# Attention and expert layer on one core: three tiles of two experts computed during the attention, PSUM tiles shared anew, all in one list schedule

## The chip, the cores and the metric

The kernel runs on one core of a Trainium2 chip. The core has five engines that run their own instruction streams side by side: TensorE (PE, matmuls; PEld is its weight load), VectorE (DVE), ScalarE (ACT), GpSimd (POOL) and SyncE (SP). All of a core's transfers share 16 DMA engines. The metric is device time in microseconds (us) of one execution; lower is better.

## The reference

Eight batches, 8 heads, 576 positions, head size 64. Two attentions are added: one over q, k and v averaged over groups of four positions (144 positions, repeated back to 576), one over a band of the positions nearer than four. The result, 4608 tokens of 512 values, goes through an expert layer: each token goes to one of eight experts.

```python
out = np.repeat(sm_attn(q_d, k_d, v_d), 4, axis=2) + sm_attn_band(q, k, v)   # |i-j| < 4
x = out.transpose(0, 2, 1, 3).reshape(4608, 512)
logits = x @ w_gate
e_idx = np.argmax(logits, axis=1)
gate_w = softmax(logits)[arange, e_idx]
eom = sigmoid(x @ w_output_gate)
for e in range(8):
    mask = e_idx == e
    h = np.maximum(x[mask] @ w1[e], 0.0)          # 512 -> 1024
    out[mask] = gate_w * eom[:, e] * (h @ w2[e])  # 1024 -> 512
```

## The kernel before

The program has two phases, and they don't overlap.

**The attention** is cut into 32 units (a batch's heads two by two: `prep`, `scores`, `values`), with a gate step after each batch (`gate`). All of it is put in as tasks with an engine, a duration and dependencies; `Plan.order` simulates a list schedule of them, and the kernel is written out in that order, so each engine runs its tasks strictly in it. A task's priority is ten times its slot plus a number from the table `AT`. A unit is, with the names that the tasks have and the lines of the profile:

- Tq, Tk: TensorE turns q and k into PSUM (L396), DVE copies them out (qT, kT, L402), POOL averages them (qs, qd, ks, kd, L410 to L418); VD: TensorE averages v (L433), ACT copies (vd, L439).
- DS, LS: the two score matmuls (L455 and L468/L478) into the one PSUM tile S (two banks; columns 0 to 290 of each bank for the band, the rest for the averaged scores). ED, EL: ACT takes exp of the two parts (L460, L484).
- V1: averaged values and their denominators (L503) into the one PSUM tile PD; V2: the band's denominators (L512), also into PD; V3: the band's values (L524) into the one tile PL. S, PD and PL have two banks each, the ring T of turned tiles has two of one bank: all eight banks.
- LND, LN: ACT takes the log of the two denominators (L537, L532), LX: their reciprocal by exp (L540). M2 and M1: DVE multiplies (xd L547, xl L554). ADD: POOL adds (xT L565), CAST: POOL casts (L568).
- Per batch: GL (logits, L601), GT, a chain of short DVE steps, RK (ranks, L633 to L639), INV (which token goes to which place, L686), acc; GX0 to GX2 turn the batch's tokens back (L706), ACT and DVE copy them (xh), `put` (L715) writes 576 rows to the table `hx_xs` in memory.

q and k come a batch at a time (one transfer each, L359, on POOL's queue), v a unit at a time on SP's queue. The weights of three experts are loaded during the attention, in three ring places.

**The experts** begin when all eight batches are in the table. `fetch(e)` gathers five tiles of 128 rows (an indirect DMA each, L774, on POOL); `turn` turns them (L785); `up` makes 64 matmuls U of 320 columns (L794), with a relu on ACT or DVE (L797, L799); `down` makes eight matmuls Y of 512 columns for each tile (L804), ACT scales (y, L806), POOL scatters the rows to the output (L807). Eight experts have five tiles each, so there are 40. Loads of w for expert e+3 stand on POOL's queue behind the scatters of expert e. A loop at the end handles experts with more than 640 tokens; it doesn't run with these inputs.

Of the kernel before, what the change touches and what calls it, by code (L numbers as in the profile page):

```python
# [58 lines left out]
class Task:  # L59

    def __init__(self, kind, slot, eng, dur, fn, deps, uses, mode, lat):
        self.kind, self.slot, self.eng, self.dur, self.fn = kind, slot, eng, dur, fn
# [4 lines left out]
class Plan:

    HOP = 0.10
    SWITCH = 0.13  # L70
# [32 lines left out]
    def order(self):  # L103
        free, mode, wait = {}, None, {}
# [7 lines left out]
        while len(seq) < len(self.tasks):  # L112
# [44 lines left out]
def kernel(  # L157
# [85 lines left out]
    r_qk = [ring(sbA, [HB, H, 8 * D], F16, f"qk{i}", 2) for i in range(2)]  # L243
# [27 lines left out]
    t_ks = add("c1", 0, "DVE", 1.0, c_ks)  # L271
# [8 lines left out]
    t_band = add("c2", 0, "POOL", 1.5, c_band)  # L280
# [9 lines left out]
    t_mk = add("c3", 0, "DVE", 1.0, c_mk, deps=[t_band])  # L290
# [28 lines left out]
    t_pv = add("c4", 0, "DVE", 4.6, c_pv, deps=[t_pb])  # L319
# [5 lines left out]
    t_wg0 = add("c5", 4, "DVE", 0.5, c_late, deps=[t_id])  # L325
# [4 lines left out]
    t_wg = add("c5", 5, "SP", 1.0, c_wg, deps=[t_wg0], lat=2.0)  # L330
# [9 lines left out]
    t_cg = add("c5", 4, "POOL", 2.0, c_gate)  # L340
# [6 lines left out]
    t_rev = add("c5", 5, "DVE", 0.6, c_rev, deps=[t_cg])  # L347
# [35 lines left out]
    def prep(u):  # L383
# [4 lines left out]
        for i, nm in enumerate("qk"):  # L388
# [32 lines left out]
            e2 = add("kd" if i else "qd", n, "POOL", 1.4 if i else 0.9, fn, deps=[ev, t_ks], uses=[xT, s2, sd])  # L421
# [5 lines left out]
        def fn(T=T):  # L427
            for blk in range(3):
                for s in range(2):
                    for h in range(2):  # L430
                        g = 2 * blk + s
                        r0 = 64 * h + 32 * s
                        nc.tensor.matmul(T.tile[r0:r0 + 32, D * blk:D * blk + D], lhsT=pv[:, g, :],  # L433
                                         rhs=vbuf.tile[:, min(g, NB - 1), h, :], start=(blk == 0), stop=True,
                                         skip_group_check=True)
# [479 lines left out]
```

## Time and profile before

| | us |
|---|---|
| median of three runs | 441.91 (437.96 to 444.44) |
| the profiled execution | 438.84, its span 437.0 |
| TensorE busy | 347.9 (80% of the span) |
| VectorE, ScalarE, GpSimd busy | 222.0 (51%), 180.7 (41%), 261.4 (60%) |
| mean granted clock of TensorE | 0.902 |

The span is the time from the first to the last instruction; 1.84 us of the execution lie around it. [...] A busy share is an average over two phases that have different limits.

### The profile page before, as it was taken

The numbers are of one execution on the slowest core, as the hardware profiler recorded it, in microseconds if no ns is written. First come the engines' busy times: TensorE is split into PE (matmuls) and PEld (weight loads), VectorE is DVE, ScalarE is ACT, GpSimd is POOL, SyncE is SP. The second block draws the span as 40 slices with busy tenths as digits, with TensorE's granted clock in tenths as the row PEclk, the third lists the DMA queues.
The fourth block names the chain that finished last, engine by engine and source line by source line (L and its number), as shares of the span: only waits on it lengthen the run. The fifth ranks groups of instructions, "written<-read, shape, count | busy, mean of one in ns | idle before, by whom it ended". The sixth has DMA issues, their size and how long they took to land.

```text
span 437.0 us, 14182 instructions
## 1 busy us (share of the span) xinstructions
PE 347.9 (80%) x6105; PEld 244.9 (56%) x6105; DVE 222.0 (51%) x550; ACT 180.7 (41%) x369; POOL 261.4 (60%) x363
## 2 busy tenths in 40 slices
PE   1268879779868968689788544699999999999990
PEld 0256657567656756567567332356565665656640
DVE  8343578387677487696967661233242332323210
ACT  1045654454545555456656420123333343343430
POOL 8375976755956668767684317517485755842330
PEclk9998997686977889989999855889999999999996
DMA  6994499961898655994330113315988989891221
GB/s 105 183 168 76 79 163 190 182 112 39 164 190 138 148 102 89 213 189 111 70 79 7 56 54 92 91 39 136 230 187 231 162 241 223 197 235 60 84 75 47
DMA packets 79113, 57.21 MB, mean 131 GB/s; under 512 B 49341, under 2 KB 71357, under 8 KB 79040
## 3 DMA queue, kind: packets, MB, share of 16 engines
q0 software_dynamic: 30240, 40.94, 46.9%
q1 hardware_dynamic: 48800, 15.26, 16.8%
q8 instruction: 50, 0.82, 0.7%
q14 instruction: 23, 0.19, 0.2%
HBM read 68.21 MB, written 15.22 MB: 191 GB/s over the span
## 4 chain that ended last, share of the span: by engine, by line
PE 39%; DVE 16%; POOL 16%; issue 12%; DMA 8%; ACT 5%; POOLq 1%; DVEq 0%; ACTq 0%
PE U L794 12%; PE Y L804 10%; PE PD L503 4%; POOL xT L565 3%; DMA w<-in_moe_w_dram 3%; DMA qk<-in_k_dram 3%; PE PD L512 3%; POOL out_dram L807 3%; DVE kT L402 2%; DVE xl L554 2%; PE T L706 2%; POOL kd L418 2%; DVE xd L547 2%; ACT r L540 2%; DVE g_og L644 2%
## 5 line engine op out<-in xcount | busy, mean ns | idle before, releaser
L807 POOL DMA_INDIRECT out_dram<-y,sidx x40 | 39.7, 993 | 64.8 <-ACT y L806 35.0
L794 PE MATMUL U<-xgT,w 128*128 128x320 f16 x512 | 75.5, 310 | 3.6 <-issue 1.4
L804 PE MATMUL Y<-w,hs 128*128 128x512 f16 x320 | 73.8, 379 | 0.0
L794 PEld LDWEIGHTS <-w 128*128 128x128 f16 x512 | 51.8, 101 | 27.1 <-issue 4.2
L799 DVE TENSOR_SCALAR hs<-U 128x320 f16<-128x320 f32 x64 | 31.4, 492 | 68.5 <-PE U L794 57.2
L565 POOL TENSOR_TENSOR xT<-xl,xd 128x576 f32<-128x576 f32 x32 | 38.7, 1210 | 24.8 <-DVE xl L558 24.2
L774 POOL DMA_INDIRECT xg<-hx_xs,gidx x40 | 40.7, 1018 | 21.3 <-issue 11.3
L797 ACT ACTIVATE hs<-U 128x320 f16<-128x320 f32 x64 | 27.9, 437 | 59.2 <-PE U L794 58.0
L806 ACT ACTIVATE y<-Y,xg 128x512 f32<-128x512 f32 x40 | 27.5, 688 | 55.7 <-PE Y L804 38.0
L804 PEld LDWEIGHTS <-hs 128*128 128x128 f16 x320 | 30.5, 98 | 31.5
L503 PE MATMUL PD<-e,vd 64*128 64x144 f32 x384 | 40.6, 352 | 5.3 <-DVE xd L547 4.3
L396 PE MATMUL T<-id,qk 72*64 72x72 f16 x1024 | 28.8, 214 | 19.3 <-DMA qk<-in_q_dram 14.0
L537 ACT ACTIVATE r<-PD 64x144 f32<-64x144 f32 x64 | 18.3, 286 | 55.9 <-PE PD L512 55.5
L547 DVE TENSOR_TENSOR xd<-PD,r 64x144 f32<-64x144 f32 x64 | 19.5, 305 | 42.0 <-ACT r L540 33.0
L410 POOL TENSOR_TENSOR ks<-kT 128x288 f32<-128x288 f16 x32 | 21.9, 685 | 28.9 <-DVE kT L402 28.7
L396 PEld LDWEIGHTS <-qk 72*64 72x64 f16 x1024 | 23.8, 124 | 26.6 <-DMA qk<-in_q_dram 14.2
L503 PEld LDWEIGHTS PD<-e,vd 64*128 64x128 f32 x384 | 32.7, 230 | 7.8 <-issue 2.8
L786 DVE COPY xgT<-T 128x1024 f16<-128x1024 f16 (+1 forms) x24 | 14.4, 602 | 42.3 <-PE T L785 39.5
L418 POOL TENSOR_TENSOR kd<-ks 64x192 f16<-64x192 f32 x64 | 32.3, 505 | 4.4
L402 DVE COPY kT<-T 128x576 f16<-128x576 f16 x32 | 24.1, 754 | 17.4 <-PE T L396 17.2
L524 PE MATMUL PL<-e,v 64*64 64x57 f32 (+1 forms) x1280 | 28.6, 232 | 1.1 <-issue 0.9
L402 DVE COPY qT<-T 128x576 f16<-128x576 f16 x32 | 23.9, 749 | 9.4 <-PE S L478 5.0
(120 smaller groups left out, 580.6 us busy)
## 6 DMA issues: line engine op xcount, KB each, us to landing
w<-in_moe_w_dram POOLq DMA_DIRECT2D x16, 1024.0 KB
v<-in_v_dram SPq DMA_DIRECT2D x128, 80.0 KB, 5.6
hx_xs<-xh SPq DMA_DIRECT2D x8, 578.2 KB, 4.8
qk<-in_q_dram POOLq DMA_DIRECT2D x7, 576.0 KB
qk<-in_k_dram POOLq DMA_DIRECT2D x7, 576.0 KB
xg<-hx_xs,gidx POOLq DMA_INDIRECT x40
out_dram<-y,sidx POOLq DMA_INDIRECT x40
qk<-in_q_dram POOLq DMA_DIRECT2D x1, 432.0 KB
```

The lines of the kernel that those rows point to most:

```text
L396: nc.tensor.transpose(t16[64 * h:64 * h + 64, HB * c:HB * c + HB], src.tile[:, 2 * hp + h, D * c:D * c + D], id16[0:HB, 0:HB])
L402: nc.vector.tensor_copy(xT.tile.rearrange("p (n c) -> p n c", c=8), T.tile.bitcast(F16)[:, 0:S].rearrange("p (c n) -> p n c", c=8))
L418: nc.gpsimd.tensor_tensor(o.rearrange("p b (s x) -> p b s x", s=2), _ap(t, [t.ap[0], [114, 3], [58, 2], [2, 32]]), _ap(t, [t.ap[0], [114, ...
L503: nc.tensor.matmul(o, lhsT=vd.tile[r, blk, D - D * h:3 * D - D * h], rhs=x, start=(blk == 0), stop=(blk == 2), skip_group_check=True)
L524: nc.tensor.matmul(p[64 * h:64 * h + 64, par, c0:c1], lhsT=vbuf.tile[r, g, h, :], rhs=et[r, h, c0:c1], start=(g == 0), stop=True, skip_gro ...
L547: nc.vector.tensor_tensor(xd.tile[r, :], PD.tile[r, h, WC:WC + SD], r_.tile[r, L2:L2 + SD], op=ALU.mult)
L565: nc.gpsimd.tensor_tensor(xT.tile[:, hp, :].rearrange("p (n m) -> p n m", m=4), xl.tile.rearrange("p (n m) -> p n m", m=4), _bc(xd.tile, 4 ...
L774: nc.gpsimd.indirect_dma_start(out=xg[:, j, :], out_offset=None, in_=xs_dram.ap(), in_offset=bass.IndirectOffsetOnAxis(ap=idx[:, c0 + j:c0 ...
L794: nc.tensor.matmul(pu[:, 0:c1 - c0], lhsT=w1sb[:, c, 128 * f:128 * f + 128], rhs=xgT[:, c, c0:c1], start=(c == 0), stop=(c == 3))
L799: nc.vector.tensor_scalar_max(hs[:, f, c0:c1], pu[:, 0:c1 - c0], 0.0)
L804: nc.tensor.matmul(py, lhsT=hs[:, f, 128 * j:128 * j + 128], rhs=w2sb[:, f, :], start=(f == 0), stop=(f == NG - 1))
L807: ins = nc.gpsimd.indirect_dma_start(out=out, out_offset=bass.IndirectOffsetOnAxis(ap=idx, axis=0), in_=y[:, j, :], in_offset=None, bounds ...
```

## The change

It does five things.

1. **Early experts.** After six of the eight batches (`SNAP` = 5) the places so far are copied (`places(gfirst, sfirst)`). Of experts 0 and 1 (`AHEAD` = 2) the first three tiles (`AJ` = 3) are then computed as tasks of the list schedule: `ahead(e)` gathers them (EG), turns them (ET, EX), makes U with 384 columns (EU, relu EH and EI), Y (EY, Ey) and scatters (ES). They take U and Y tiles from the ring PL, and hidden and output tiles from the q and k buffers, which therefore have 128 rows. `room` raises the counts of the two experts to 384, so that later tokens don't fall into these tiles. The expert phase then gathers and computes two tiles for experts 0 and 1, with U in one cut of 256 columns, and five for the others.
2. **PSUM.** PD is gone. V1 goes into the tile PL beside V3, and PL has two tiles now; V2 writes the band's denominators into S, over the band's scores that EL has read. The list schedule sees S as two rings, one for each half of the columns.
3. **CAST** goes from POOL to ACT.
4. **The start.** The ones beside vd come from TensorE and ACT in place of 26 DVE memsets; q and k of batch 0 come in three parts (2, 2 and 4 heads) and not in two (2 and 6).
5. **The planner's numbers.** Transfers take their place in a model of one queue (`dma`, `LAND`); some durations and all of `AT` are new.

```diff
-    r_S = ring(psA, [128, 2, 512], F32, "S", 1)
-    r_PL = ring(psA, [128, 2, 512], F32, "PL", 1)
-    r_PD = ring(psA, [128, 2, 512], F32, "PD", 1)
+    S_s = psA.tile([128, 2, 512], F32, tag="S", name="S", bufs=1)
+    r_Sd = fixed_ring([S_s])
+    r_Sl = fixed_ring([S_s])
+    r_PL = ring(psA, [128, 2, 512], F32, "PL", 2)
+    r_xg = ring(gpool, [128, CAPJ, XW // 2], I32, "xg", 3)
+    r_xt = ring(sbA, [128, 4, 128 * AJ], F16, "xt", 1)
...
+            if t.dma:
+                moved = max(moved, t.end) + t.dma
+                t.lat = moved + self.LAND - t.end
...
-        v1 = add("V1", u, "PE", 0.6, fn, deps=[d["ed"], d["tvd"]], uses=[e, vd, PD], mode=64128, lat=0.2)
+        v1 = add("V1", u, "PE", 0.8, fn, deps=[d["ed"], d["tvd"]], uses=[e, vd, PL], mode=64128, lat=0.2)
...
-        v2 = add("V2", u, "PE", 0.45, fn, deps=[d["el"], v1], uses=[e, PD], mode=6464, lat=0.2)
+        v2 = add("V2", u, "PE", 0.45, fn, deps=[d["el"]], uses=[e, Sl], mode=6464, lat=0.2)
...
-        v3 = add("V3", u, "PE", 1.08, fn, deps=[v2], uses=[e, vbuf, PL], mode=6464, lat=0.2)
+        v3 = add("V3", u, "PE", 0.8, fn, deps=[d["el"], v1], uses=[e, vbuf, PL], mode=6464, lat=0.2)
...
-        l1 = add("LN", u, "ACT", 0.66, fn, deps=[v2, v1], uses=[PD, r_])
+        l1 = add("LN", u, "ACT", 0.66, fn, deps=[v2], uses=[Sl, r_])
...
-        l2 = add("LND", u, "ACT", 0.58, fn, deps=[v1, v2], uses=[PD, r_])
+        l2 = add("LND", u, "ACT", 0.58, fn, deps=[v1], uses=[PL, r_])
...
-        ca = add("CAST", u, "POOL", 0.7, lambda: nc.gpsimd.tensor_copy(x16.tile[:, hp, :], xT.tile[:, hp, :]),
+        ca = add("CAST", u, "ACT", 0.67, lambda: nc.scalar.copy(x16.tile[:, hp, :], xT.tile[:, hp, :]),
...
+                nc.vector.tensor_scalar(room, C.tile[0:1, 0:AHEAD], scalar1=-1.0, scalar2=128.0 * AJ, op0=ALU.mult,
+                                        op1=ALU.add)
+                nc.vector.tensor_scalar(room, room, scalar1=0.0, scalar2=None, op0=ALU.max)
+                nc.vector.tensor_tensor(cum[0:1, 0:AHEAD], cum[0:1, 0:AHEAD], room, op=ALU.add)
...
     load_qk(0, 0, 2)
-    load_qk(0, 2, H)
+    load_qk(0, 2, 4)
+    load_qk(0, 4, H)
...
+    def ahead(e):
+        n = NU + 1 + 2 * e
+        xg, xt, hb, yb = Buf(r_xg), Buf(r_xt), Buf(r_qk[0]), Buf(r_qk[1])
+        w = 128 * AJ
...
+        got = [add("EG", n, "POOL", 1.0, lambda j=j: gather(xg.tile[:, j, :], gfirst[:, col + j:col + j + 1], S * (SNAP + 1)),
+                   deps=[first["snap"], first[SNAP]], uses=[xg], lat=2.3) for j in range(AJ)]
...
+        for i in range(NG // 2):
+            U = Buf(r_PL)
...
+                    for c in range(4):
+                        nc.tensor.matmul(U.tile[:, k, 0:w], lhsT=wts[e][0][:, c, 128 * f:128 * f + 128],
+                                         rhs=xt.tile[:, c, :], start=(c == 0), stop=(c == 3), skip_group_check=True)
+            up = add("EU", n, "PE", 1.3, fn, deps=turned + [t_w[e]], uses=[xt, U], mode=128, lat=0.2)
...
+            dn = add("EY", n, "PE", 1.72 * len(js), fn, deps=made, uses=[hb, Y], mode=128, lat=0.2)
...
+                add("ES", n, "POOL", 1.0, lambda j=j: scatter(y(j), sfirst[:, col + j:col + j + 1], True),
+                    deps=[ev], uses=[yb], lat=2.0)
...
+        parts = [(e, AJ if e < AHEAD else 0) for e in range(E)]
...
+            j0 = parts[e][1]
+            for j in range(j0, CAPJ):
+                col = CAPJ * (E - 1 - e) + j
+                gather(xgs[e][:, j - j0, :], gidx[:, col:col + 1], N)
...
+        cuts = [0, 128 * nj] if nj <= 4 else [0, 64 * nj, 128 * nj]
```

Three places show what the new order is. The first is TensorE in the middle of the attention, from a unit's V1 on; PD, PL and S are the PSUM tiles, e the exponentials. Before:

```order
L503 MATMUL PD_3953<-e_3778,vd1_95 128x144 x6
L512 MATMUL PD_3953<-e_3778,on_l_77 64x291 x4
L524 MATMUL PL_3978<-e_3778,v_3244 64x60 x4
L524 MATMUL PL_3978<-e_3778,v_3244 64x57 x12
L524 MATMUL PL_3978<-e_3778,v_3244 64x60 x4
```

Now:

```order
L521 MATMUL PL_3935<-e_3729,vd1_99 128x144 x6
L530 MATMUL S_107<-e_3867,on_l_77 64x291 x4
L337 MATMUL T_3955<-v_3480,pv_76 32x64 x12
L542 MATMUL PL_3935<-e_3729,v_3107 64x60 x4
L542 MATMUL PL_3935<-e_3729,v_3107 64x57 x12
L542 MATMUL PL_3935<-e_3729,v_3107 64x60 x4
```

V1 writes PL and V2 writes S for another unit (e_3867, the next one) than V1 and V3 (e_3729); before, all three were one unit's.

The second is ACT in the middle of the attention, about one unit. r is the tile of logs and reciprocals, vd the averaged values, x16 what CAST makes. Before (LND and LN of PD, LX, vd, the next LND, LN and LX, then EL and ED):

```order
L537 ACTIVATE r_2800<-PD_2760 64x144 x2
L532 ACTIVATE r_2800<-PD_2760 128x582
L540 ACTIVATE r_2800<-r_2800 128x726
L439 COPY vd0_94<-T_2855 128x3x64
L537 ACTIVATE r_2898<-PD_2873 64x144 x2
L532 ACTIVATE r_2898<-PD_2873 128x582
L540 ACTIVATE r_2898<-r_2898 128x726
L484 ACTIVATE e_2978<-S_2890 128x2x291
L460 ACTIVATE e_2978<-S_2890 128x2x216
```

Now (LN of S, CAST, vd, LND of PL, ED, EL, a gate step, LX, CAST and the next LN):

```order
L550 ACTIVATE r_3458<-S_107 128x582
L586 CAST x16_3188<-xT_3142 128x576
L457 COPY vd0_98<-T_3486 128x3x64
L555 ACTIVATE r_3458<-PL_3502 64x144 x2
L478 ACTIVATE e_3551<-S_107 128x2x216
L502 ACTIVATE e_3551<-S_107 128x2x291
L665 ACTIVATE g_ez_3615<-g_ogs_3571 96x6
L558 ACTIVATE r_3458<-r_3458 128x726
L586 CAST x16_3188<-xT_3142 128x576
L550 ACTIVATE r_3646<-S_107 128x582
```

LN and LND, which stood side by side, now stand apart, with CAST, vd and other tasks between them; CAST is new on this engine.

The third is POOL at the end of the attention. xT is ADD, xg a gather, out a scatter, w a load. Before:

```order
L565 TENSOR_TENSOR xT_5289<-xl_5499,xd_5496 128x576
L568 CAST x16_5352<-xT_5289 128x576
L565 TENSOR_TENSOR xT_5289<-xl_5549,xd_5546 128x576
L568 CAST x16_5352<-xT_5289 128x576
L774 DMA xg_5687<-hx_xs,gidx_92 128x257 x5
L774 DMA xg_5703<-hx_xs,gidx_92 128x257 x5
L774 DMA xg_5751<-hx_xs,gidx_92 128x257 x5
L807 DMA out_0_dram<-y_5724,sidx_93 4608x512 x5
```

Now:

```order
L787 DMA xg_5231<-hx_xs,gfirst_95 128x257
L787 DMA xg_5338<-hx_xs,gfirst_95 128x257 x3
L583 TENSOR_TENSOR xT_5184<-xl_5423,xd_5353 128x576
L583 TENSOR_TENSOR xT_5184<-xl_5490,xd_5463 128x576
L583 TENSOR_TENSOR xT_5184<-xl_5530,xd_5527 128x576
L792 DMA out_0_dram<-qk1_5611,sfirst_96 4608x512 x3
L792 DMA out_0_dram<-qk1_5817,sfirst_96 4608x512 x2
L787 DMA xg_5850<-hx_xs,gidx_92 128x257
L792 DMA out_0_dram<-qk1_5817,sfirst_96 4608x512
L787 DMA xg_5850<-hx_xs,gidx_92 128x257
L787 DMA xg_5857<-hx_xs,gidx_92 128x257 x2
L787 DMA xg_5880<-hx_xs,gidx_92 128x257 x5
```

The gathers of the early experts stand before the last three ADDs; their six scatters stand before the expert phase's gathers, but for the last one, which stands between the first and the second of these. TensorE's early matmuls (EU, EY) all stand behind the last V3, between the steps of the last batches' gates.

## Rows read from the trace of the kernel before

**Rows 1.** Busy time by engine and granted clock in stretches, us from the span's start:

```profile
core 0: us, PE busy (x) PEld busy (x) DVE busy (x) ACT busy (x) POOL busy (x), PEclk, DMA share, GB/s
34.00:248.00 214.00, 175.02 (x4703) 137.53 (x4698) 150.64 (x355) 116.53 (x248) 148.06 (x218) 0.88 0.66 122
65.00:70.00 5.00, 3.89 (x43) 2.69 (x45) 3.92 (x12) 1.34 (x3) 2.70 (x3) 0.50 1.22 195
200.00:240.00 40.00, 34.01 (x995) 26.72 (x984) 28.81 (x71) 25.02 (x54) 26.59 (x41) 1.00 0.25 63
248.00:271.00 23.00, 9.07 (x84) 6.21 (x79) 9.87 (x39) 3.29 (x6) 9.00 (x9) 0.57 0.22 61
271.00:298.00 27.00, 23.41 (x129) 13.21 (x128) 6.07 (x12) 6.21 (x13) 11.85 (x12) 0.83 0.25 74
298.00:426.00 128.00, 127.88 (x848) 77.67 (x845) 38.28 (x74) 47.89 (x92) 69.24 (x71) 1.00 0.74 173
```

**Rows 2.** Timeline of TensorE, V1 of unit 1:

```profile
34.98 1.81 PE L503 MATMUL PD<-e,vd 64*128 64x144 f32 x12
```

**Rows 3.** Timeline of TensorE, V1 of units 24 and 31, V3 of unit 31:

```profile
200.98 1.01 PE L503 MATMUL PD<-e,vd 64*128 64x144 f32 x12
...
244.62 1.01 PE L503 MATMUL PD<-e,vd 64*128 64x144 f32 x12 [0.69 <-DVE xd L547]
...
246.34 1.30 PE L524 MATMUL PL<-e,v 64*64 64x60 f32 x40
```

**Rows 4.** Waits of TensorE, 34 to 248 us: in total, times, longest:

```profile
PE S L468 <- ACT e L460: 9.5, 5, 2.2
...
PE PD L503 <- DVE xd L547: 4.3, 5, 1.2
```

**Rows 5.** Timeline of ACT in unit 24:

```profile
202.71 0.58 ACT L537 ACTIVATE r<-PD 64x144 f32<-64x144 f32 x2 [1.18 <-PE PD L512]
...
203.31 0.66 ACT L532 ACTIVATE r<-PD 128x582 f32<-128x582 f32 x1
...
204.06 0.82 ACT L540 ACTIVATE r<-r 128x726 f32<-128x726 f32 x1
...
206.26 0.66 ACT L484 ACTIVATE e<-S 128x582 f32<-128x582 f32 x1 [1.18 <-PE PL L524]
...
206.81 0.53 ACT L460 ACTIVATE e<-S 128x432 f32<-128x432 f32 x1
```

**Rows 6.** Groups of instructions by line: count, busy, mean ns, idle before:

```profile
L568 POOL CAST x<-xT 128x576 f16<-128x576 f32 x32 | 21.4, 670 | 2.1
...
L439 ACT COPY vd<-T 128x192 f32<-128x192 f32 x32 | 10.0, 312 | 11.4 <-PE T L433 9.1 <-PE PD L503 2.2
```

**Rows 7.** Timeline, the start:

```profile
3.97 0.91 POOL L359 DMA_DIRECT2D qk<-in_q_dram  x1
...
19.98 1.17 PE L396 MATMUL T<-id,qk 72*64 72x72 f16 x32 [2.85 <-DMA qk<-in_k_dram]
...
33.49 0.35 PE L455 MATMUL S<-qd,kd 128*128 128x144 f16 x4 [3.09 <-POOL xT L565]
```

**Rows 8.** Timeline, from the last gate step to the first U:

```profile
261.86 1.12 POOL L774 DMA_INDIRECT xg<-hx_xs,gidx  x1 [9.43 <-DVE most L770]
...
264.83 0.61 PE L785 MATMUL T<-id,xg 128*128 128x128 f16 x4 [4.88 <-DMA xg<-hx_xs,gidx]
...
271.06 1.27 PE L794 MATMUL U<-xgT,w 128*128 128x320 f16 x4
```

**Rows 9.** The chain of waits in the expert phase: start, us, what:

```profile
297.89 8.69 PE U L794 x64
306.58 1.73 PE Y L804 x8
...
316.33 8.69 PE U L794 x64
...
376.00 13.92 DMA w<-in_moe_w_dram
```

**Rows 10.** Timeline, ACT's last instruction:

```profile
425.92 0.69 ACT L806 ACTIVATE y<-Y,xg 128x512 f32<-128x512 f32 x1 [1.04 <-PE Y L804]
```

More of the change, by code (lines that the diff above doesn't have):

```diff
@@ L237 @@
     sidx = cst.tile([128, NC], I32)
+    none = cst.tile([128, NC], F32)
+    gfirst = cst.tile([128, NC], I32)
+    sfirst = cst.tile([128, NC], I32)
+    room = cst.tile([1, AHEAD], F32)
     vd_s = [cst.tile([128, 3, 3 * D], F32, tag=f"vd{i}", name=f"vd{i}") for i in range(2)]
@@ L270, in c_ks @@
             nc.vector.memset(t, 0.0)
-    t_ks = add("c1", 0, "DVE", 1.0, c_ks)
+    t_ks = add("ks", 0, "DVE", 1.0, c_ks)
     def c_band():
@@ L279, in c_band @@
                                     base=3 - off, pattern=[[-1, 66]], channel_multiplier=1)
-    t_band = add("c2", 0, "POOL", 1.5, c_band)
+    t_band = add("band", 0, "POOL", 1.5, c_band)
     def c_mk():
@@ L318, in c_pv, with means, c_ones @@
             nc.vector.tensor_copy(pv[64:128, g, m:n], pb[64:128, o, m + 2 + o:n + 2 + o])
-    t_pv = add("c4", 0, "DVE", 4.6, c_pv, deps=[t_pb])
+    t_pv = add("pv", 0, "DVE", 2.4, c_pv, deps=[t_pb])
+    on = Buf(r_T)
+    def means(T, rhs):
+        for blk in range(3):
+            for s in range(2):
+                for h in range(2):
+                    g = 2 * blk + s
+                    r0 = 64 * h + 32 * s
+                    nc.tensor.matmul(T[r0:r0 + 32, D * blk:D * blk + D], lhsT=pv[:, g, :],
+                                     rhs=rhs(min(g, NB - 1), h), start=(blk == 0), stop=True, skip_group_check=True)
+    t_on = add("on", 0, "PE", 0.5, lambda: means(on.tile, lambda g, h: on_l), deps=[t_pv], uses=[on], mode=32, lat=0.2)
+    def c_ones():
+        for t in vd_s:
+            for o in (0, 2 * D):
+                nc.scalar.copy(t[:, :, o:o + D], on.tile[:, 0:3 * D].rearrange("p (b d) -> p b d", d=D))
+    t_ones = add("ones", 0, "ACT", 1.3, c_ones, deps=[t_on], uses=[on])
     def c_late():
@@ L324, in c_late @@
         nc.vector.memset(cum, 0.0)
-    t_wg0 = add("c5", 4, "DVE", 0.5, c_late, deps=[t_id])
+    t_wg0 = add("late", 4, "DVE", 0.5, c_late, deps=[t_id])
     def c_wg():
@@ L339, in c_gate @@
         nc.gpsimd.iota(colv, pattern=[[REG // 128, E], [1, CAPJ]], base=REG // 128, channel_multiplier=0)
-    t_cg = add("c5", 4, "POOL", 2.0, c_gate)
+    t_cg = add("gate", 4, "POOL", 2.0, c_gate)
     def c_rev():
@@ L346, in c_rev @@
         nc.vector.memset(acc, 0.0)
-    t_rev = add("c5", 5, "DVE", 0.6, c_rev, deps=[t_cg])
+    t_rev = add("rev", 5, "DVE", 0.6, c_rev, deps=[t_cg])
     qb, vb = {}, {}
@@ L425, in prep @@
         vbuf, vt = vb[u]
[L427 to L435, printed above, removed]
-        tv = add("VD", n, "PE", 0.65, fn, deps=vt + [t_pv], uses=[T, vbuf], mode=32, lat=0.2)
+        tv = add("VD", n, "PE", 0.5, lambda T=T: means(T.tile, lambda g, h: vbuf.tile[:, g, h, :]), deps=vt + [t_pv], uses=[T, vbuf], mode=32, lat=0.2)
         d["vd"] = vd
@@ L711, in fn @@
                     xh.tile[:, 2 * i:2 * i + 2, 0:Dm], tp.tile.bitcast(F16)[0:TB, :].rearrange("p (j n) -> p j n", j=2))
-            rows.append(add(f"xh{i}", n, "ACT" if i else "DVE", 1.13 if i else 0.69, fn, deps=[gx], uses=[tp, xh]))
+            rows.append(add(f"xh{i}", n, "ACT" if i else "DVE", 1.03 if i else 0.69, fn, deps=[gx], uses=[tp, xh]))
         def fn():
@@ L716, in fn @@
                               xh.tile.bitcast(I32))
-        add("put", n, "SP", 0.8, fn, deps=[t6] + rows, uses=[xh], lat=2.5)
+        first[b] = add("put", n, "SP", 0.8, fn, deps=[t6] + rows, uses=[xh], dma=1.3)
     wts = {}
@@ new lines, in gather, with scatter @@
+    def gather(dst, idx, rows):
+        nc.gpsimd.indirect_dma_start(
+            out=dst, out_offset=None, in_=xs_dram.ap()[0:rows, :],
+            in_offset=bass.IndirectOffsetOnAxis(ap=idx, axis=0), bounds_check=rows - 1, oob_is_err=False)
+    def scatter(y, idx, group):
+        ins = nc.gpsimd.indirect_dma_start(
+            out=out, out_offset=bass.IndirectOffsetOnAxis(ap=idx, axis=0),
+            in_=y, in_offset=None, bounds_check=N - 1, oob_is_err=False)
+        if group:
+            tc.declare_no_dep(ins.ins, group="out_scatter", reason="the rows differ")
+            tc.add_to_no_dep_group("out_scatter", ins.ins)
@@ L745 @@
+    first["snap"] = add("snap", NU, "DVE", 0.55, lambda: places(gfirst, sfirst), deps=[first["acc"]])
+    for e in range(AHEAD):
+        ahead(e)
     with tc.manual_schedule():
@@ L828 @@
         count()
-        xts[0] = tiles(CAPJ)
-        for j0 in range(0, CAPJ, 2):
-            turn(xgs[0], xts[0][0], CAPJ, j0)
+        xts[0] = tiles()
+        nj = CAPJ - parts[0][1]
+        for j0 in range(0, nj, 2):
+            turn(xgs[0], xts[0][0], nj, j0)
         for e in range(E):
```

210 lines of the change are left out of this document (130 added, 80 removed), and 13 rows, old and new, of the table AT.

## The prediction

> **What bounds the kernel now.** I read the stretches of busy time and granted clock first, then the timelines at their borders, then TensorE's waits, and last the chain of waits. The reader is to see two phases with different limits. In the expert phase TensorE is full: 127.88 of 128 us busy at clock 1.00 [rows 1]; an expert is 18.44 us there (316.33 - 297.89), 64 U at 8.69 us and five tiles of Y at 1.73 us [rows 9], so only less work, or a part done elsewhere, shortens it. In the attention TensorE is not full, 175.02 of 214 us, and its clock is 0.88 [rows 1]. A unit takes 6.99 us there ((244.62 - 34.98) / 30), 7.22 us in units 1 to 24 and 6.23 us in the last seven [rows 2, 3]; V1 alone takes 1.81 us in unit 1, where the clock is low, and 1.01 us in unit 24 [rows 2, 3]. What ends TensorE's idle time is mostly a PSUM tile: the next unit's band scores wait for ED (9.5 us in 5 waits), V1 waits for M2 to leave PD (4.3 us in 5) [rows 4]. Between the phases TensorE does little: 9.07 of 23 us at clock 0.57 [rows 1], while the last batch's gate ends, the first gather goes out (261.86), lands (264.83) and is turned, until the first U at 271.06 [rows 8]. So the time before is a sum of four stages: 34.98 to the second V1, 209.64 for 30 units, 26.44 from the last V1 (244.62) to the first U, 154.86 from there to the last y (425.92 [rows 10]), then 11.08 of span for the last scatters and the end, and 1.84 around the span: 438.84, the profiled execution, 0.7% below the median of 441.91. My sum is made against 438.84.
>
> **Start: 22 us instead of 34.98.** Before, the first q load is issued at 3.97, behind POOL's constants; Tk of unit 1 waits 2.85 us for the k of six heads and begins at 19.98; the DS ahead of V1 of unit 1 waits 3.09 us for POOL, where an ADD stands ahead of the kd that it needs [rows 7]. Now the loads of four heads stand ahead of the constants, about 3.2 us earlier. ADD of unit 0 has gone behind that kd, and that DS behind V1. In the new order V1 of unit 1 stands behind Tk of units 2 and 3, which need the last four heads. If all q and k land 3.2 us earlier, that is at 16.8. Behind it come Tk of unit 2 (half of 1.17 [rows 7]), LS, EL (0.66 [rows 5]), V2 and Tk of unit 3, with copies and hand-overs between them about 5 us by my estimate. That gives 22. Bounds: 19, if the last heads land earlier than so, and 28.7 (34.98 - 3.2 - 3.09), if only the two plain gains arrive. DVE's 26 memsets gone lie in front of nothing that I price.
>
> **Attention: 30 units at 6.5 us, 195 instead of 209.64.** Removed: the wait for M2 at V1 (PL has two tiles now), and the tie of LN to V1. POOL loses CAST, 670 ns a unit [rows 6]. Added: CAST on ACT, the same size by the planner's number, and a new tie. DS and LS of the next unit cannot enter S before LN has read it, since V2 now writes there; and in the built order V3 waits for LND in 26 of the 32 units, DS for the LN of the unit before in 23 of 26 waits, LS for ED in 14. So S goes through scores, exp, V2, LN in one cycle, and ACT is in that cycle. Summed in ACT's new order from the rows: LN 0.66, vd 0.31, LND 0.58, ED 0.53, EL 0.66, LX 0.82 [rows 5, 6], CAST 0.67, a gate step of about 0.2 now and then, one V1 that ACT waits for (1.01 at full clock [rows 3]) with 0.3 of hand-over, and about 0.67 for a second CAST or a V2: 6.4 us. At low clock V1 costs 0.8 more [rows 2]: 7.2. [...] From below, TensorE's own work is 34.01 / 40 x 6.23 = 5.3 us a unit at clock 1.00 [rows 1, 3]; with some 0.6 of hand-overs 5.9. From above, nothing gained and the CAST partly on the path: 7.2. So 177 to 216. Who is queued behind what: on ACT, CAST waits for ADD on POOL, and behind it stands LN of the next unit, for which DS waits. Transfers don't set this pace: their share is 0.66 of 214 us, 141 us, and stretches reach 1.22 [rows 1], so they fit in 116 us.
>
> [...]
>
> **From the last V1 to the first U: 40 us instead of 26.44.** All early EU and EY stand behind the last V3, in the gaps of the last two batches' gates. V1 to the end of the last V3 took 3.02 (246.34 + 1.30 - 244.62 [rows 3]). Early U: 64 of 384 columns at 8.69 / 64 x 384 / 320 = 0.163, 10.4 us; early Y: 6 tiles x 1.73 = 10.4 us [rows 9]. The gates' own matmuls: of the 9.07 us [rows 1] about 6.7, the rest was the turning of the first expert. 27.5 us of work in a row, with 2.4 us of stalls, since the gates' DVE chain (before, 9.43 us of it showed as POOL's wait ahead of the first gather [rows 8]) now runs under the early work. Then POOL: two gathers and the last early scatter, about 1.1 each [rows 8], landing 2.97 (264.83 - 261.86), the turns and copies: 7.1. Sum 40.0. Bounds 35 (no stalls, the gathers hidden under EY) and 47 (clock at 0.75 in the stretch).
>
> **Experts: 131.6 instead of 154.86.** Experts 0 and 1 keep two tiles: 32 U of 256 columns 3.5 and two Y tiles 3.46 [rows 9], turns 0.6 each [rows 8]: 8 us each, 16 together. The six others keep what they took, 425.92 - 316.33 = 109.6 [rows 9, 10]. Expert 0 took 26.83 before, 8.4 more than the second, at clock 0.83 [rows 1]; TensorE comes from early work now, so I put 4. Two short experts leave less cover for w of expert 3, a load of 13.92 us [rows 9], and for ten scatters and gathers on POOL ahead of it: 2. Bounds 127 and 137.
>
> The end (11.08) and what lies around the span (1.84) stay. **Sum: 22 + 195 + 40 + 131.6 + 12.9 = 401.5.** I say 402.
>
> **Rivals.** [...]
>
> *The new ties eat the gain.* S's wait for LN and V3's for LND take the place of PD's; the pace stays 7.0: 416.5. For it: one S tile as before, and ACT with one task more; against it: ACT was busy 116.53 of 214 us only [rows 1].
>
> *Early work gives little.* Stalls in the early U and Y (two PL tiles, relu on the same ACT and DVE that finish the gates) and a wait for w at expert 3: 47 and 137, 413.5.
>
> *Slower than before.* ACT's queue: CAST stands ahead of LN and waits for ADD on POOL; POOL's lag would then go round S, LN, DS and back to POOL each unit. At 8.0 us a unit this is 446.5. It decides above 7.75 ((438.84 - 401.5) / 30 + 6.5). Against it: POOL is relieved of those 670 ns a unit [rows 6], and was busy 148.06 of 214 us with them [rows 1], so its lag should shrink.
>
> **How the numbers follow.** Forecast 0.45 (390 to 413), clock up 0.20, ties 0.20, little from early work 0.10, slower 0.05. The range reaches from 382, below the clock rival, to 425, beyond the ties with a start of 28.7: about one case in ten is left out on either side. 2% of the median, 8.8 us, is about what a measurement of this kernel can tell from no change: faster means below 433, same 433 to 451. Only the last rival and combinations of the worst bounds reach there: 0.90, 0.05, 0.05.
>
> **What would show it.** Right: V1 of unit 1 near 22; V1s 6.5 us apart, and TensorE's waits headed by DS for LN and V3 for LND, none for M2; some 40 us from the last V1 to the first U of the expert phase, with 27 us of TensorE's work in them; experts 0 and 1 at 8 us, the others at 18.4. Wrong: a pace near 5.9 with clock 1.00 throughout, or near 7; gaps between the early EU that add up to more than 6 us; an expert 3 that begins with several us of wait for w.

## The result, and the profile after

The changed kernel takes 417.47 us (median of four runs, 415.32 to 419.73), the kernel before 442.41 in the same comparison: a ratio of 0.945, 95% interval 0.936 to 0.954. The profiled execution took 415.32 us, its span 413.5. Ratios here and below leave out executions that took over 1.5% longer than the fastest of their kernel. The forecast of 402 was 3.7% too low, inside its range of 382 to 425.

First the borders of the stages: V1 of units 1 and 31, the first U of the expert phase, and ACT's last y. Timelines of the changed kernel (start, us, engine, line):

```profile
22.30 1.01 PE L521 MATMUL PL<-e,vd 64*128 64x144 f32 x12
...
233.09 1.81 PE L521 MATMUL PL<-e,vd 64*128 64x144 f32 x12
...
272.48 5.82 PE L910 MATMUL U<-xgT,w 128*128 128x256 f16 x32 [0.94 <-DVE xgT L902]
...
401.83 0.69 ACT L922 ACTIVATE y<-Y,xg 128x512 f32<-128x512 f32 x1 [1.04 <-PE Y L920]
```

They answer to [rows 2, 3, 8, 10]. Set beside the prediction's sum:

| stage, us | before | forecast | after |
|---|---|---|---|
| to V1 of unit 1 | 34.98 | 22 | 22.30 |
| 30 units | 209.64 | 195 | 210.79 |
| last V1 to first U | 26.44 | 40 | 39.39 |
| first U to last y | 154.86 | 131.6 | 129.35 |
| end, and around the span | 12.92 | 12.9 | 13.49 |

Four terms came within 2.3 us. The whole error is one term: a unit takes 7.03 us, where 6.99 was to become 6.5.

TensorE's waits in those 30 units, in total, times, longest:

```profile
PE PL L542 <- issue: 9.7, 9, 3.1
PE T L423 <- issue: 3.8, 3, 2.1
PE T L337 <- issue: 2.4, 1, 2.4
PE S L496 <- issue: 2.1, 1, 2.1
PE T L704 <- DVE kT L429: 1.9, 1, 1.9
PE S L486 <- ACT e L478: 1.7, 8, 0.4
PE S L473 <- issue: 1.6, 1, 1.6
...
PE PL L542 <- ACT r L555: 0.5, 2, 0.3
```

Against [rows 4]: the wait of LS for ED went from 9.5 us to 1.7, and V1's for M2 is gone. Added up over the whole view, waits for other engines went from 28.0 us to 15.1, which is the 0.4 us a unit that was forecast. But waits put down to "issue", to nothing that the profile shows, went from 9.4 to 20.6; they are called stops below. They took back most of what was won. No transfer of q, k, v or w is among the waits.

Where these stops stand shows in stretches with and without the weights' loads, which are issued at 54.7, 99.6 and 156.3 us (columns as in [rows 1]; PEclk is the granted clock, a share of TensorE's full speed):

```profile
54.50:79.80 25.30, 18.66 (x503) 14.54 (x501) 15.19 (x38) 14.89 (x31) 15.83 (x23) 0.92 1.06 193
79.80:95.20 15.40, 14.36 (x403) 11.40 (x399) 11.30 (x31) 10.24 (x23) 9.25 (x14) 0.92 0.49 90
95.20:127.50 32.30, 23.73 (x632) 18.38 (x631) 20.53 (x52) 18.79 (x40) 21.28 (x32) 0.88 0.95 165
127.50:153.60 26.10, 23.56 (x653) 18.62 (x649) 18.45 (x49) 17.77 (x38) 16.21 (x24) 0.88 0.63 116
153.60:184.70 31.10, 25.45 (x642) 19.84 (x641) 19.99 (x54) 18.37 (x37) 21.33 (x32) 0.84 1.00 173
```

The borders are V1s. With a transfers' share of about 1, 3, 4 and 4 units take 8.4, 8.1 and 7.8 us each, and TensorE is busy 73 to 82% of the time. Between the loads it is busy 90 to 93%, and the other 19 units take 6.42 us each ((210.79 - 88.8) / 19), from 5.1 between the first two loads to 6.9 behind the last.

One such stop, from all engines' timeline:

```profile
120.60 0.61 PE L542 MATMUL PL<-e,v 64*64 64x60 f32 x25
...
121.85 0.66 ACT L586 CAST x<-xT 128x576 f16<-128x576 f32 x1
...
123.92 0.42 POOL L440 TENSOR_TENSOR qd<-qs 128x144 f16<-128x144 f32 x1
124.27 0.59 PE L542 MATMUL PL<-e,v 64*64 64x57 f32 x12 [3.05 <-issue]
...
125.12 0.62 DVE L565 TENSOR_TENSOR xd<-PL,r 64x144 f32<-64x144 f32 x2 [3.24 <-PE PL L542]
```

V3 breaks off after 25 of its 40 matmuls and goes on 3.05 us later with the same operands: no engine or tile is waited for. Counted over the trace's 12,260 records of TensorE's instructions, the ten stops of this sort, of 0.73 to 3.05 us, behind the first load stand here (instructions already run; time at which TensorE goes on; end of the last transfer of the kind "instruction" ahead of it):

```
2475   58.92   57.63        5273  124.27  122.90
2728   65.42   63.91        6035  142.30  140.99
2984   71.89   70.37        7307  167.58  165.96
3237   78.66   77.12        7817  181.17  179.82
4763  110.86  109.45
5019  117.60  116.04
```

They are 253 to 256 instructions apart, or a multiple of about 254, and TensorE goes on 1.3 to 1.6 us after the end of an instruction transfer. There are 50 such transfers on queue 8 in the page (queue and kind: transfers, MB, share of the 16 engines), so 16 KB each; the 12,260 records over 50 transfers are 245 for each, near the spacing of the stops:

```profile
q8 instruction: 50, 0.82, 0.8%
```

Two of the ten are mixed: the profile puts the waits at 2475 (1.26 us) and 6035 (1.30 us) down to DVE. The transfers ahead of the ten took 0.88 to 1.12 us, no longer than the others on this queue, so it is not their length that makes the stops. The one ahead of the end of the stop above ran from 121.90 to 122.90 and began when TensorE had stood still for 0.7 us. What it waited for until then no view shows; the experiments test whether it is the weights.

Spacing and count would fit if each of these transfers brought TensorE its next block of instructions; that is my inference from the two numbers, and no view names the engine that a transfer is for. In the expert phase no wait behind the first U is put down to "issue", though the share is 0.79 there too (291 to 402 us): the instruction transfers are 17 to 21 us apart there, in the attention mostly 4 to 8.

The theory to test, called PAGES below: TensorE's blocks of instructions arrive late behind the weights. Its rival, TIES, is the prediction's, that the new ties eat the gain: the cycle over S, LN and DS sets the pace of 7.0, which is the number that came out (416.5 forecast, 415.32 measured).

### The profile page after: what moved, and what is told of

Its sections match the earlier page's. It is cut to its first block, busy times and chain, and to the rows that moved or that the text cites. A ratio compares the mean times of both kernels' runs of the same rounds, so it can differ in the third digit from the quotient of the medians.

```text
span 413.5 us, 14230 instructions
## 1 busy us (share of the span) xinstructions
PE 346.9 (84%) x6130; PEld 243.1 (59%) x6130; DVE 207.6 (50%) x530; ACT 201.4 (49%) x405; POOL 242.7 (59%) x333
## 4 chain that ended last, share of the span: by engine, by line
PE 55%; issue 16%; DVE 13%; POOL 7%; ACT 5%; DMA 1%; POOLq 0%; DVEq 0%
PE U L910 13%; PE Y L920 10%; PE PL L521 5%; PE PL L542 4%; PE S L530 4%; PE T L423 3%; POOL out_dram L792 3%; PE T L337 2%; PE T L619 2%; DVE xd L565 2%; DVE xl L572 2%; PE T L901 2%; ACT r L558 1%; PE S L473 1%; DVE qT L429 1%
## 5 line engine op out<-in xcount | busy, mean ns | idle before, releaser
L910 PE MATMUL U<-xgT,w 128*128 128x320 f16 (+1 forms) x448 | 63.2, 302 | 1.6 <-DVE xgT L902 0.9
L920 PE MATMUL Y<-w,hs 128*128 128x512 f16 x272 | 63.0, 379 | 0.5 <-DVE hs L915 0.5
L910 PEld LDWEIGHTS <-w 128*128 128x128 f16 x448 | 44.8, 100 | 19.8 <-issue 2.5
L915 DVE TENSOR_SCALAR hs<-U 128x320 f16<-128x320 f32 (+1 forms) x56 | 26.7, 482 | 57.7 <-PE U L910 52.7
L913 ACT ACTIVATE hs<-U 128x320 f16<-128x320 f32 (+1 forms) x56 | 23.8, 429 | 44.3 <-PE U L910 31.1
L521 PE MATMUL PL<-e,vd 64*128 64x144 f32 x384 | 38.0, 337 | 0.1
L565 DVE TENSOR_TENSOR xd<-PL,r 64x144 f32<-64x144 f32 x64 | 19.4, 304 | 35.1 <-ACT r L558 23.7
L542 PEld LDWEIGHTS PL<-e,v 64*64 64x64 f32 x1280 | 26.8, 148 | 16.5 <-issue 12.0
L423 PEld LDWEIGHTS <-qk 72*64 72x64 f16 x1024 | 23.6, 119 | 19.9 <-issue 11.4
L437 POOL TENSOR_TENSOR qs<-qT 128x288 f32<-128x288 f16 x32 | 21.3, 667 | 19.0 <-DVE qT L429 15.9
L521 PEld LDWEIGHTS PL<-e,vd 64*128 64x128 f32 x384 | 30.1, 216 | 3.8 <-DVE xd L565 0.9
L550 ACT ACTIVATE r<-S 128x582 f32<-128x582 f32 x32 | 20.9, 654 | 17.6 <-PE S L530 14.1
L902 DVE COPY xgT<-T 128x1024 f16<-128x1024 f16 (+1 forms) x20 | 12.1, 611 | 33.1 <-PE T L901 33.1
```

What stands on the lines that cost most here:

```text
L437: nc.gpsimd.tensor_tensor(s2.tile[:, 0:S // 2], pairs[:, :, 0], pairs[:, :, 1], op=ALU.add)
L521: nc.tensor.matmul(o, lhsT=vd.tile[r, blk, D - D * h:3 * D - D * h], rhs=x, start=(blk == 0), stop=(blk == 2), skip_group_check=True)
L542: nc.tensor.matmul(p[64 * h:64 * h + 64, par, c0:c1], lhsT=vbuf.tile[r, g, h, :], rhs=et[r, h, c0:c1], start=(g == 0), stop=True, skip_gro ...
L565: nc.vector.tensor_tensor(xd.tile[r, :], PL.tile[r, h, WC:WC + SD], r_.tile[r, L2:L2 + SD], op=ALU.mult)
L910: nc.tensor.matmul(pu[:, 0:c1 - c0], lhsT=w1sb[:, c, 128 * f:128 * f + 128], rhs=xgT[:, c, c0:c1], start=(c == 0), stop=(c == 3))
L915: nc.vector.tensor_scalar_max(hs[:, f, c0:c1], pu[:, 0:c1 - c0], 0.0)
```

## The experiments

All but one keep the order of the instructions that they don't name; the planner still plans the old tasks, and instructions are moved, cut or added when they are written out. `plan.then[kind, slot]` runs a function right behind a task. Ratios are to the kernel before on the same chip. Its median was 442.41 beside the changed kernel, 434.16 on the chip of w_less, w_quiet, w_thin and w_again, 435.17 on that of cast_pool, start_old, no_ahead and b_less, and 443.08 on that of after_same, w_mix, b_quiet and pl_one, so times in us compare best within such a group. In the last column are TensorE's stops and its other waits in the 30 units.

| | ratio (95%) | V1 of unit 1 | 30 units | to first U | experts | stops, other waits |
|---|---|---|---|---|---|---|
| changed | 0.945 (0.936, 0.954) | 22.30 | 210.79 | 39.39 | 129.35 | 20.6, 15.1 |
| after_same | 0.942 (0.938, 0.946) | 22.66 | 210.02 | 38.04 | 130.68 | 20.2, 12.5 |
| w_less | 0.904 (0.898, 0.911) | 23.81 | 195.36 | 38.68 | 126.70 | 8.5, 19.3 |
| w_quiet | 0.928 (0.923, 0.933) | 23.67 | 201.86 | 39.32 | 127.42 | 15.6, 14.6 |
| w_thin | 0.933 (0.926, 0.940) | 22.82 | 200.50 | 39.22 | 127.40 | 10.5, 19.6 |
| w_mix | 0.921 (0.917, 0.925) | 23.87 | 202.85 | 38.15 | 129.47 | 13.7, 19.2 |
| w_again | 0.965 (medians) | 22.10 | 215.34 | 38.17 | 126.77 | 22.7, 16.4 |
| cast_pool | 0.949 (0.941, 0.956) | 22.03 | 209.87 | 38.56 | 127.61 | 16.1, 19.1 |
| start_old | 0.959 (0.953, 0.965) | 26.71 | 201.87 | 39.26 | 127.61 | 13.8, 18.4 |
| no_ahead | 0.974 (0.967, 0.980) | 21.78 | 202.31 | 28.74 | 149.10 | 17.7, 16.7 |
| pl_one | 1.029 (1.024, 1.035) | 22.99 | 217.83 (29 units) | 69.38 (from unit 30) | 129.12 | 8.7, 27.9 |
| before | | 34.98 | 209.64 | 26.44 | 154.86 | 9.4, 28.0 |
| b_less | 1.002 (0.998, 1.006) | 34.19 | 217.23 | 26.77 | 149.02 | 3.0, 35.2 |
| b_quiet | 1.021 (1.017, 1.025) | 35.21 | 220.92 | 27.17 | 156.18 | 2.9, 39.8 |

The columns of times are each kernel's profiled execution; that of start_old and of no_ahead was 6 us below its median, so their attention is 207 to 208 us in the median if the difference lies there. They load the weights as the changed kernel does and still show 202 us, so the column for 30 units doesn't tell w_quiet, w_thin or w_mix from the changed kernel by itself. The ratios do, for w_quiet and w_mix.

**w_less: fewer bytes of weights.**

```diff
+    def weights_less(e):
+        nc.gpsimd.dma_start(wts[e][0][:, 0:1], moe_w1[e][0:128]...)
+        nc.gpsimd.dma_start(wts[e][1][:, 0:2], moe_w2[e][0:256]...)
```

> The changed kernel with a quarter of the early weights loaded: of each of the experts 0 to 2 one of four blocks of w1 and two of eight of w2; the rest of the tiles is set to zero by two memsets each on GpSimd. The order of all other instructions is the same. Theory PAGES (TensorE stands still when a block of 256 of its own instructions arrives late behind the weight transfers; those stops, 17 us in the attention, and slower units while the weights come make the pace 7.03 where it is 6.4 between the loads): the stops that are put down to nothing fall to under 5 us, units take 6.4 to 6.6 us, 400 to 406. Rival TIES (the cycle over S, LN and DS and the shared PL set the pace; the stops only stand where another wait would): 7.0 us stay, 413 to 418.

Measured 394.32 us, ratio 0.904, shorter than the expected 400 to 406; the kernel leaves out three quarters of these weights, so its output is not the layer's. A unit takes 6.51 us; the stops are 8.5 us, not under 5. TensorE's waits now begin with kd, probably delayed by the memsets on POOL:

```profile
PE S L476 <- POOL kd L448: 4.5, 7, 1.3
PE PL L545 <- issue: 3.3, 3, 2.5
PE T L426 <- issue: 3.3, 3, 1.9
```

and the clock of the 30 units is 0.94:

```profile
23.80:219.20 195.40, 166.50 (x4678) 130.11 (x4674) 140.44 (x359) 130.97 (x272) 143.79 (x210) 0.94 0.61 115
```

Of the 15.4 us by which the attention is shorter than in the changed kernel's trace, about 12.1 are stops, 7.9 are busy time of TensorE (174.4 to 166.5 for the same matmuls, at clock 0.90 and 0.94), and 4.2 came back as waits. The kernel before is 1.9% apart in the two comparisons, so part of the 15.4 can be the chip; the ratio, 4 points lower, is free of that. TIES is out: with the cycle over S untouched the pace is the forecast 6.5.

**w_quiet: the same bytes, later.**

```diff
+    for e in range(3):
+        plan.then["ADD", 22 + e] = [lambda e=e: weights(e)]
```

> The changed kernel with the loads of all three experts' weights behind ADD of units 22, 23 and 24, in the stretch in which the transfers' share was 0.17 to 0.26; all other instructions in the same order. PAGES: the loads run alone and so are shorter (about 11 us each), 4 or 5 blocks of instructions come late in place of 9, between 185 and 225 us; 405 to 411, with a wait of the early U for the weights if they land after 237. TIES: 415 to 419.

404.10 us, ratio 0.928, better than expected. The work is complete, and without loads ahead of unit 21 the first 20 units take 6.55 us each (23.67 to 154.65; in the changed kernel 7.00). On the same chip w_again, whose loads in these units are the changed kernel's, takes 7.06; between the two, stops go from 13.3 us to 4.0, other waits from 9.8 to 13.2. The rest of the attention pays for some of it, with six stops of 0.6 to 2.8 us between 176 and 211 us, behind the loads' issue at 168 to 182; four or five were expected. The first row is w_again, the others are w_quiet:

```profile
22.10:163.30 141.20, 118.04 (x3226) 91.99 (x3226) 91.55 (x229) 88.70 (x183) 96.30 (x147) 0.89 0.81 142
...
23.70:154.70 131.00, 113.00 (x3230) 88.18 (x3226) 91.43 (x229) 88.59 (x184) 90.52 (x142) 0.93 0.65 121
154.70:225.50 70.80, 57.37 (x1450) 43.53 (x1448) 46.39 (x129) 42.87 (x89) 44.58 (x64) 0.88 0.90 161
```

**w_thin: the same bytes in 24 pieces.**

```diff
+    for i in range(24):
+        plan.then["ADD", 2 + i] = [lambda i=i: weights_in(i // 8, i % 8)]
```

> The changed kernel with the weights of three experts in 24 pieces, one behind each ADD of units 2 to 25; all other instructions in the same order. GpSimd issues 24 transfers in place of 6, some 15 us more of its time. PAGES: the transfers never stand more than a few us deep, stops under 6 us, 401 to 408. TIES: 416 to 420 (GpSimd has more to do).

404.21 us, ratio 0.933. The stops fall to 10.5 us, not under 6, and kd is waited for 5.1 us, probably since GpSimd issues four times as many transfers. The direction is that of PAGES, but the interval meets the changed kernel's, so no gain is shown.

**w_again: more bytes where there were few.**

```diff
+    for e in range(2):
+        plan.then["ADD", 24 + 2 * e] = [lambda e=e: weights_again(e)]
```

> The changed kernel which loads the weights of experts 0 and 1 a second time into the same tiles, behind ADD of units 24 and 26, where transfers are few; all other instructions in the same order. PAGES: stops of 2 to 3 us appear between 195 and 225 us, 256 instructions apart, two for each load: 422 to 428. TIES: 416 to 419, no stops there.

419.08 us in the median (413.26 to 421.95) against 434.16 for the kernel before, 0.965 by the medians; the two shortest of its four runs are at 0.952 and 0.961. That is 0.7 to 2 points over the changed kernel and, with so few runs, not clear of noise; 422 to 428 was too much. The traces say more. From 180 to 225 us the share goes from 0.32 to 0.91, and two stops of more than 1 us appear that the changed kernel doesn't have there:

```profile
209.28 0.57 PE L545 MATMUL PL<-e,v 64*64 64x57 f32 x24 [1.71 <-issue]
216.59 0.90 PE L545 MATMUL PL<-e,v 64*64 64x60 f32 x39 [1.11 <-issue]
```

They stand after 9088 and 9342 instructions, 254 apart, but they are two and shorter than expected, not four; a wait for kd of 3.38 us stands beside them. The place is that of PAGES, the size only in part.

**after_same: the changed kernel again.** No edit.

> The changed kernel itself, on the chip of the other experiments, for a direct comparison and a second trace. By the ratio of 0.945 it takes about 410 us here. PAGES: the stops come again, 14 to 21 us in the attention, while the weights land (55 to 80, 100 to 125, 157 to 182 us), 256 instructions apart; the attention of 30 units takes 202 to 211 us.

416.63 us, ratio 0.942; this chip was the slower one, so the 410 was wrong and the ratio right. Eight of the ten stops come again after the same instructions (2475, 2728, 2984, 4763, 5273, 6035, 7307 and 7817), 3237 and 5019 do not, and one of 0.88 us is new at 6545; all stops are 20.2 us.

**w_mix: pieces where nothing waits for their issue.**

```diff
+    for i, u in enumerate((7, 10, 13, 16, 19, 21, 22, 23, 24, 25, 26, 27)):
+        plan.then["kd", u] = [lambda i=i: weights_in(i // 4, i % 4)]
```

> The changed kernel with the weights of three experts in 12 pieces, each behind a kd, so that no kd waits behind an issue; one piece every third unit first, one in each unit from 21 to 27, where transfers are few; all other instructions in the same order. PAGES: stops under 9 us and waits for kd under 3 us: 399 to 404 here, ratio 0.918 to 0.930. TIES: no better than the changed kernel.

408.54 us beside 416.63 for the changed kernel on the same chip: ratios 0.921 (0.917 to 0.925) and 0.942 (0.938 to 0.946), 2.2% better than it and the lowest ratio of a complete kernel here, though its interval meets that of w_quiet. The ratio came as expected, and kd is waited for 0.9 us only. The expected stops didn't come: 13.7 us remain, one of 3.04 us at unit 23, where the pieces come one a unit.

**cast_pool: CAST back on GpSimd.**

```diff
+            nc.gpsimd.tensor_copy(x16.tile[:, hp, :], xT.tile[:, hp, :])
+        plan.then["ADD", u] = [fn]
```

> The changed kernel with CAST on GpSimd, right behind each ADD, and not on ScalarE; all other instructions in the same order. PAGES: ScalarE's queue doesn't set the pace, so within 3 us of the changed kernel, or a little slower since GpSimd has 21 us more: ratio 0.94 to 0.955. TIES (the cycle of S over ScalarE's queue): 0.67 us less in the cycle of each unit, 10 to 20 us faster, ratio 0.90 to 0.92.

0.949, within the interval of the changed kernel. No gain or loss by moving CAST shows, and TensorE's waits in the changed kernel have none for LN, so the slower rival (CAST ahead of LN) had its mechanism wrong. Whether ScalarE's shorter cycle would gain by itself stays open: TensorE waits 7.2 us for kd here, for 1.2 in the changed kernel, since GpSimd has CAST again.

**start_old: the loads of batch 0.**

```diff
+    plan.then["id", 0] = [lambda: load_first(0, 2), lambda: load_first(2, H)]
```

> The changed kernel with q and k of batch 0 loaded in two parts (2 and 6 heads), behind the first constants on GpSimd; all other instructions in the same order. The start's gain of 12.7 us is then split: if the loads make it, V1 of unit 1 comes 6 to 9 us later and the time with it; if the order of ADD, kd and DS makes it, under 3 us.

V1 of unit 1 comes at 26.71, 4.4 us later, between the two cases; the ratio is 0.959. The loads make a third of the start's 12.7 us, so two thirds are the rest of the change at the start (ADD behind kd, DS behind V1, the ones without memsets). These were not taken apart.

**no_ahead: no early experts.**

```diff
+            if t.kind in ("EG", "ET", "EX", "EU", "EH", "EI", "EY", "Ey", "ES", "snap", "CNT", "room"):
+                continue
```

> The changed kernel without its early experts: their tasks are planned and then not written out, so all other instructions stand in the same order; all eight experts have five tiles in the expert phase. By the stages of the changed kernel's trace the early part takes 13 us more between the last V1 and the first U and saves 25 us behind it: 12 to 14 us slower than the changed kernel, ratio to the kernel before about 0.975. If the early work gave little, as one rival had it: under 5 us slower, ratio 0.955.

0.974 as expected: the early work is worth 3 points, 12 to 13 us. By the stages of the two traces it costs 10.7 us ahead of the first U and saves 19.8 behind, 9 us in all.

**b_less and b_quiet: the same two cuts in the kernel before.** The diffs are those of w_less and w_quiet.

> The kernel before with a quarter of the early weights loaded, as the same cut in the changed kernel (the rest set to zero by memsets on GpSimd; the order of all else is the same). PAGES: here the stops are 10 us in all and waits for other engines 28, so less is won than the 15 us of the changed kernel's attention: 6 to 10 us, ratio 0.977 to 0.986. If the transfers themselves and not TensorE's own instructions were late: as much as in the changed kernel, 14 us and more, ratio under 0.97. TIES: ratio 0.995 to 1.0.

> The kernel before with the three experts' weights loaded behind ADD of units 22 to 24, in the same order otherwise and without memsets. PAGES in both kernels alike: ratio 0.980 to 0.985, as in the changed kernel (0.928 to 0.945). If the stops of the kernel before stand where TensorE would wait for other engines anyway, as the cut in its weights suggests: 0.993 to 1.003.

Ratios 1.002 and 1.021, so PAGES' forecasts for this kernel (0.977 to 0.986, 0.980 to 0.985) were wrong: b_less came near TIES' number (0.995 to 1.0), and b_quiet lies above both of its cases. The stops fall from 9.4 us to 3.0 and 2.9, and nothing is won: other waits grow from 28.0 to 35.2 and 39.8, and over the 30 units the clock is 0.85 where it was 0.89, with TensorE busy 7 us longer. kd is waited for 11.4 and 11.2 us (5.7 before), in b_less perhaps for its memsets, but b_quiet has none. The first 20 units of b_quiet, without loads, take 7.13 us (35.21 to 177.8), against 7.25 before:

```profile
35.20:177.80 142.60, 117.77 (x3130) 90.70 (x3126) 96.05 (x221) 75.49 (x161) 98.81 (x148) 0.87 0.56 105
```

In these units stops fall from 8.6 us to 1.8 and other waits grow from 16.4 to 22.8, nearly as much. The same cut gave the changed kernel 0.45 us a unit, from 7.00 to 6.55. The rest of b_quiet's loss is in the units beside the loads, where TensorE waits 5.1 us for v. So in the kernel before the stops mostly stood where TensorE would have waited for ED, kd or M2 anyway.

**pl_one: one PL tile.**

```diff
-    r_PL = ring(psA, [128, 2, 512], F32, "PL", 2)
+    r_PL = ring(psA, [128, 2, 512], F32, "PL", 1)
```

> The changed kernel with one PL tile in place of two (two banks stay empty); the order is planned anew for it with the same numbers. If the second tile carries the gain of the new PSUM order, V1 waits for M1 of the unit before: 0.5 to 1 us a unit, 15 to 30 us, ratio 0.98 to 1.01. If the ties cost what the second tile gives: ratio 0.94 to 0.955.

454.68 us, 1.029, slower than both cases. In the new order all the early U and Y stand ahead of V1 of unit 31, so this V1 no longer marks the end of 30 like units:

```profile
240.82 1.81 PE L521 MATMUL PL<-e,vd 64*128 64x144 f32 x12
...
284.61 1.01 PE L521 MATMUL PL<-e,vd 64*128 64x144 f32 x12 [0.78 <-ACT qk L861]
```

The table's row therefore ends at V1 of unit 30. These 29 units take 7.51 us each, after_same's 6.87 (22.66 to 222.01). That is 18.5 us, the size of the first case, but V1's waits for M1 are 4.7 us of it; TensorE also waits more for kd and for exp (5.3 and 11.7 us), at a clock of 0.86:

```profile
PE S L473 <- POOL kd L445: 5.3, 4, 1.8
PE PL L521 <- DVE xl L576: 4.7, 5, 1.9
```

From V1 of unit 30 to the first U it takes 69.38 us in place of 48.71, with one tile for the early U and Y to write and empty by turns. The order was planned anew with numbers made for two tiles, so how much of the 38 us is the second tile itself is not shown.

## Why the forecast was right in four terms and 16 us off in one

- **Start: right in the number, by luck** (22.30 for 22). I built the 22 on the landing of the loads, and they carry 4.4 of the 12.7 us. In the changed kernel TensorE waits for no q or k behind 7.1 us and is busy 10.59 of the 12 us ahead of this V1.
- **Attention: the failing step** is the sentence that transfers don't set this pace because 141 us of them fit into 116. That was a mean over 214 us. The transfers come in three bursts with a share of about 1 (0.95 to 1.06), and what they hold up is no operand that the waits show: TensorE breaks off in mid-run and goes on 1.3 to 1.6 us after an instruction transfer. That these carry its own instructions is inferred. The 6.5 us in the sum was a choice between the 6.4 and the 7.2 that I summed from ScalarE's order at full and at low clock, and no run shows it as a term; in its place the changed kernel showed 7.03, and 6.42 between the loads, 6.55 in w_quiet's first units and 6.51 in w_less, where there were no bursts. The term missed is some 15 us of bursts: 12 of stops, the rest busy time at a lower clock (0.90 beside 0.94). That the stops bring the clock down is not shown: in b_less and b_quiet they went and the clock fell. The mechanism of the 6.5 was not borne out either. Its sign, waits headed by DS for LN and V3 for LND, didn't come: 0.5 us in all for LND, none for LN. In w_less the 6.5 is 5.55 us of TensorE's own work, 0.28 of stops and 0.64 of many small waits, nearer to the lower bound that I summed from TensorE (5.3 and 0.6) than to a cycle through ScalarE.
- **The rival that gave the right number was wrong.** At 7.0 us a unit it said 416.5. But the ties cost next to nothing that TensorE's waits show (0.5 us for LND, none for LN), and with the ties untouched the pace fell with the weights. Only runs that cut or moved the weights could tell the two apart.
- **Waits removed: right in size.** 0.4 of the 0.5 us a unit did go (28.0 to 15.1 us of waits for engines). In the kernel before the stops mostly stood beside such waits; with the waits gone they came on the path. That is where the new order's gain in the attention went: with a quarter of the weights the two kernels are at 1.002 and 0.904 (435.52 and 394.32 us), with all of them at 1 and 0.945, which is 24 us.
- **Last V1 to first U and the experts: right**, 39.39 for 40 and 129.35 for 131.6, and in their parts. Beside the terms of the sum in brackets, TensorE is busy 30.6 of the 39.4 us (30.5: 27.5 and the 3.0 from V1 to V3's end), waits 8.1 for the first gathers and their turning (7.1), and stalls 0.5 in the early U (2.4). Experts 0 and 1 take 18.3 us (20), the other six 111.0 (111.6); the 4 us put there, about half of expert 0's 8.4 at clock 0.83, were an estimate, and the clock was 0.88 from 272.5 to 291 us. Expert 3 does not wait for its w, so the 2 us put there were not needed; expert 2 took 19.6 us, not 18.4.
- **Early work gives little** was wrong: no_ahead shows 3 points for it. (Its sum is 413.9, not 413.5.)
- **Clock up**, the faster rival (given 0.20), did not come by itself: the granted clock was 0.90 over the 30 units, where it was 0.89 before. It was 0.94 in w_less.

Left open: in both traces of the changed kernel V3 of unit 30 goes in bits with stops of 0.4 us while the early gathers are issued, and the last two V1s are 10.6 us apart, in w_again and w_mix 10.6 and 9.9; in w_less, w_quiet, w_thin, cast_pool and start_old they are 5 to 7 apart. What makes the difference was not tried.

## What to carry to other kernels

A mean share of the transfers hides bursts (0.72 over the 30 units here, 0.95 to 1.06 while the weights loaded): read it in stretches of the length of one load, and look whether the busy engine stops in the middle of a run of like instructions. When waits are taken away, ask what stood in their shadow; here it was 20.6 us of stops in which the engine waited for no operand that the profile shows. Large loads that nobody needs soon were better given in pieces here, by 2%, at places of the issuing queue behind which nothing urgent stands (w_mix). In the kernel before, where other waits stood at the same places, moving the loads won nothing.

## What was not expected of the hardware

While weights were loaded, two loads of 1 MB at a time beside q, k and v, TensorE stopped in mid-run for up to 3.1 us, at the same instruction counts in both traces of the changed kernel for eight of ten stops; with a quarter of the weights (w_less) all stops together fell from 20.6 us to 8.5. The instruction transfer of 16 KB ahead of the end of such a stop took 0.88 to 1.12 us, no longer than others on its queue; in the stop shown above it began 0.7 us after TensorE had stopped. And the loss was not only stops: on one chip, for the same matmuls of the first 20 units, TensorE was busy 118.0 us with the bursts (w_again) and 113.0 without (w_quiet), at clock 0.89 and 0.93.
